# An attention kernel with a long convolution beside it: transfers of at most 128 KB, and rows of k fetched once

## The chip, the cores and the metric

The kernel runs on one core of a Trainium2 chip. The metric is device time in microseconds of one execution. A measurement of a kernel is the median of several runs; the kernel before took 1098.95 us in the median of three (1097.54 to 1100.45).

The core has these engines, named here as the profile names them: PE multiplies matrices (PEld loads its weights), ACT applies functions, DVE does vector arithmetic, POOL and SP do little arithmetic here and issue transfers between the chip's memory and the core. The transfers themselves are moved by 16 DMA engines, which all queues share.

## What is computed

Two independent parts, written side by side into one output.

```python
def _A_ref(x, wq, wk, wv, wo):          # x [1, 2048, 512], 32 heads of 16
    q = heads(x @ wq); k = x @ wk; v = x @ wv      # one k and one v for all heads
    scores = einsum("bhqd,bkd->bhqk", q, k) * 16 ** -0.5
    o = einsum("bhqk,bkd->bhqd", softmax(scores), v)
    return concat_heads(o) @ wo

def _B_ref(q, k, v, shift_k, ssm_k, ssm_D):        # each [1, 2048, 512]
    k_shift = sum(k shifted down by i rows * shift_k[:, i] for i in range(4))
    kv = k_shift * v
    y = causal long convolution of kv with ssm_k, per channel (by FFT) + kv * ssm_D
    return q * y

out = concatenate([a, b], axis=-1)                 # [1, 2048, 1024]
```

## The kernel before, in words

**Attention** runs from the start to the end. Its 1024 tiles are taken in one fixed order by `attend`. For each, PE multiplies scores into a PSUM tile s (L781), ACT takes the exponential into p (L789), and PE multiplies p with v into accumulators f (L801), some tiles later. DVE empties the accumulators into ao every 16 tiles (L817, L818) and SP stores them (od, L820). The queries of the next group of four heads (st) are read back from memory by SP (L748), 20 tiles before they are used.

**The convolution and the projections are filler.** They are written as generators (`conv_pe`, `conv_short`, `conv_dve`, `rest_of_q`, `wo_heads`, `wo_part`). A planner, `_Fill`, lets them put a few instructions behind each attention tile, by credits of PE and DVE time per tile; `yield WAIT, n` makes a generator wait some tiles, as an allowance for a load that it has just issued. The order of every engine's instructions is therefore fixed when the program is built. At run time each engine works through its own list in order and waits on semaphores.

**Where the bytes of the filler go.** The convolution is done as a transform over 2048 positions, split 128 x 16: a row of a tensor is one of 16 positions m, on 128 partitions. Channels are taken in two blocks (blk) of CB = 256.

- `short_load`, `window` and `short_products` make kv of a block in eight steps m2 of two rows. For two rows of output with four taps, five rows of k are needed; `window` fetches those five into one of three buffers inside kk, so that each row of k is fetched two or three times. The first windows reach back before the block's rows 0: those rows are rows 13 to 15 of the partition before, fetched in two pieces, with zeros on partition 0.
- `table` loads the cosines and sines (ff forward, fi backward), 256 KB for each step; `short_products` also loads v, `backward` loads q and stores the result r.
- `long_load` loads hin, the long filter of a block, in two transfers of 1 MB. `long_forward` transforms it.
- All of these are issued by POOL, in the order of its list. A transfer takes the next of eight semaphores in turn (DMASW0 to DMASW7), and waits for the one that had this semaphore before.
- SP issues the attention's transfers and, among them, those of the projections: the store of two quarters of x (xd, L701) and their reload (xT, L737), 1 MB each; the loads of the output weights (wof, L876), of the head outputs and their scales (of, r: L853, L862), and the stores of projected rows (wp, L909). SP and ACT have eight semaphores of their own (DMAHW0 to DMAHW7), used in the same way.

Of the kernel before, what the change touches and what calls it, by code (L numbers as in the profile page):

```python
# [8 lines left out]
F32 = mybir.dt.float32  # L9
# [10 lines left out]
P = 128  # L20
S = 2048
# [75 lines left out]
class _Emit:  # L97
# [160 lines left out]
    def table(self, n, m2):  # L258
        t = self.w.tile([P, 2, 2, P], F32, tag="ft", bufs=FT, name=self.nm(n))
        self.nc.gpsimd.dma_start(t, self.I[n][:, 2 * m2 : 2 * m2 + 2])  # L260
        return t
# [22 lines left out]
    def long_load(self, blk):  # L284

        nc = self.nc
        hin = self.w.tile([P, 2, S], F32, tag="in", bufs=1, name=self.nm("hin"))
        for ct in range(2):
            c0 = blk * CB + ct * P
            nc.gpsimd.dma_start(hin[:, ct, :], self.I["B_ssm_k"][c0 : c0 + P, :])  # L290
        return hin
# [28 lines left out]
    def short_load(self, blk):  # L320
        nc, w = self.nc, self.w
        cs = slice(blk * CB, (blk + 1) * CB)
        tpb = w.tile([P, 4, CB], F32, tag="tp", bufs=1, name=self.nm("tpb"))
        for i in range(4):
            nc.gpsimd.dma_start(tpb[:, i, :], self.skd[i : i + 1, cs].broadcast_to([P, CB]))
        kk = w.tile([P, 3, 5, CB], F32, tag="in", bufs=1, name=self.nm("kk"))
        for m2 in range(2):
            self.window(kk, blk, m2)
        return tpb, kk

    def window(self, kk, blk, m2):

        nc, k, cs = self.nc, kk[:, m2 % 3], slice(blk * CB, (blk + 1) * CB)
        n = max(0, 3 - 2 * m2)
        if n:
            nc.gpsimd.memset(k[0:1, 0:n, :], 0.0)
            for a, b in ((1, 16), (16, P)):
                nc.gpsimd.dma_start(k[a:b, 0:n, :], self.kr[a - 1 : b - 1, 16 - n : 16, cs])
        nc.gpsimd.dma_start(k[:, n:5, :], self.kr[:, 2 * m2 - 3 + n : 2 * m2 + 2, cs])

    def short_products(self, blk, tpb, kk):
# [3 lines left out]
        for m2 in range(8):  # L345
            yield from self.after(*[("x", blk, m2 - AHEAD)] * (m2 >= AHEAD))
            if m2 + 2 < 8:
                self.window(kk, blk, m2 + 2)
            r = slice(2 * m2, 2 * m2 + 2)
            v = self.s2("v")  # L350
            nc.gpsimd.dma_start(v, self.vr[:, r, cs])
# [6 lines left out]
            nc.vector.tensor_tensor(a, kx(3), tap(3), ALU.mult)  # L358
            for i in (2, 1, 0):
                t = self.s2("t")  # L360
                yield 0, 700
                nc.vector.tensor_tensor(t, kx(i), tap(i), ALU.mult)  # L362
                yield 0, 700
                nc.vector.tensor_tensor(a, a, t, ALU.add)  # L364
# [31 lines left out]
    def backward(self, blk, cx, places):  # L396
# [6 lines left out]
        def load(m2):  # L403
            if m2 > 1:
                ft[m2] = self.table("fi", m2)
            q[m2] = self.s2("q")
            nc.gpsimd.dma_start(q[m2], self.qr[:, 2 * m2 : 2 * m2 + 2, cs])
# [4 lines left out]
        for m2 in range(8):  # L412
# [14 lines left out]
            nc.gpsimd.dma_start(self.orr[:, 2 * m2 : 2 * m2 + 2, D + blk * CB : D + (blk + 1) * CB], r)  # L427
# [225 lines left out]
    def prologue(self):  # L653
# [45 lines left out]
        for c in range(2, 4):  # L699
            self.k_rows(c, cut[c])  # L700
            nc.sync.dma_start(self.xd[c - 2], self.xT[c])  # L701
# [8 lines left out]
    def rest_of_q(self):  # L710
# [5 lines left out]
        for c in range(4):  # L716
# [128 lines left out]
    def heads(self, G):  # L845
# [7 lines left out]
        nc.sync.dma_start(o, od[0])  # L853
# [8 lines left out]
        nc.sync.dma_start(r, rows.unsqueeze(1).broadcast_to([8, DH, 512]))  # L862
# [36 lines left out]
    def wo_part(self):  # L899
        nc, w, I = self.nc, self.w, self.I  # L900
        xr = self.out.rearrange("b (c p i) d -> (b c) p i d", c=4, p=P, i=4)
        for c in range(3):
            yield from self.after(("oc", 4 * c + 3))
            for i in (0, 2):
                b = yield from self.wo_rows(i, range(4 * c, 4 * c + 4), 1400)
                for r in range(2):
                    t = self.s2("wp", (512,))
                    nc.vector.tensor_scalar(t, b[r], 1 / (OS * WS), None, ALU.mult)
                    nc.sync.dma_start(xr[c][:, i + r, 0:D], t)  # L909
# [305 lines left out]
```

## Time and profile before

| | |
|---|---|
| median of three runs | 1098.95 us (1097.54 to 1100.45) |
| the profiled execution | 1102.16 us, of which its span is 1100.4 us |
| mean granted clock of PE | 0.986 |
| moved by queue q0 (POOL's transfers) | 40.89 MB, 11.5% of 16 engines' span |
| moved by queue q1 (SP's) | 43.50 MB, 12.4% |
| from issue to landing, median | ff 4.6 us (256 KB), v 5.0 us (256 KB), kk 5.8 us (640 KB), hin 7.9 us (1 MB) |

The profile is taken from one execution. An engine's busy share is an average over stages with different limits: up to about 700 us PE carries attention and filler, from 700 to 850 us ACT is busy without a break, and in the last 250 us both kinds of stretch alternate. In 40 slices of 27.5 us, in tenths of busy time (DMA: of the 16 engines; GB/s: what they moved):

```profile
PE   6798889899999999999997999988888999899886
ACT  3596879799899899999988899999999999999984
DMA  7326432512312111123325422110101331111101
GB/s 230 112 83 203 138 120 64 187 59 70 121 30 68 61 52 59 45 70 120 123 92 172 164 78 71 46 40 20 41 20 31 111 98 50 52 37 30 36 4 42
```

"Issue" in the waits and in the chain is time in which an engine waited for nothing that the profile shows.

### The profile page before, as it was taken

The page shows a single profiled execution, that of the slowest core. Times are in us where ns is not written, and L with a number is a line of the kernel's source. Part 1 is how long each engine was busy: PE and PEld are TensorE (multiplying, and loading weights), DVE is VectorE, ACT ScalarE, POOL GpSimd, SP SyncE. Part 2 cuts the span into 40 slices and gives each one's busy share as a digit, 9 for nine tenths or more (in the row PEclk, how much of TensorE's full clock was granted, in tenths as well). Part 3 has the DMA queues.
Part 4 walks back from the last instruction along what each step waited for, and adds up shares of the span by engine and source line. Part 5 has one row for each costly group of instructions (what it writes and reads, how often), then busy time and mean ns, then how long its engine had stood idle before and what let it go on. Part 6 is the DMA issues. An engine that isn't in the chain of part 4 may idle for free.

```text
span 1100.4 us, 65958 instructions
## 1 busy us (share of the span) xinstructions
PE 988.4 (90%) x30907; PEld 597.8 (54%) x30907; DVE 681.7 (62%) x994; ACT 979.9 (89%) x1038; POOL 104.6 (10%) x158
## 2 busy tenths in 40 slices
PE   6798889899999999999997999988888999899886
PEld 4355556565555665665664566544444666555452
DVE  3755657788589788888877853699995211111132
ACT  3596879799899899999988899999999999999984
POOL 3212211000100000012222200000000210000000
PEclk8999999999999999999999999999999999999998
DMA  7326432512312111123325422110101331111101
GB/s 230 112 83 203 138 120 64 187 59 70 121 30 68 61 52 59 45 70 120 123 92 172 164 78 71 46 40 20 41 20 31 111 98 50 52 37 30 36 4 42
DMA packets 52002, 89.48 MB, mean 81 GB/s; under 512 B 11612, under 2 KB 34186, under 8 KB 50700
## 3 DMA queue, kind: packets, MB, share of 16 engines
q1 hardware_dynamic: 38316, 43.50, 12.4%
q0 software_dynamic: 11648, 40.89, 11.5%
q8 instruction: 243, 3.98, 1.5%
q10 hardware_dynamic: 1760, 0.81, 0.3%
q14 instruction: 35, 0.29, 0.1%
HBM read 60.16 MB, written 25.02 MB: 77 GB/s over the span
## 4 chain that ended last, share of the span: by engine, by line
ACT 45%; PE 36%; issue 11%; DVE 7%; DMA 1%; ACTq 0%; SPq 0%; DVEq 0%
ACT p L789 44%; PE f L801 16%; PE s L781 9%; PE f L221 9%; PE f L306 1%; DVE sp L142 1%; PE f L204 1%; DMA wqf<-in_A_wq 1%; DVE xT L540 1%; DVE gm L651 1%; DVE cut L619 0%; PE x L528 0%; DVE sp L256 0%; DVE gn L640 0%; PE x L204 0%
## 5 line engine op out<-in xcount | busy, mean ns | idle before, releaser
L789 ACT ACTIVATE p<-s 128x1024 f32<-128x1024 f32 x1024 | 968.1, 1050 | 86.0 <-PE s L781 78.3
L801 PE MATMUL f<-p,vx 64*32 64x256 f32 x16384 | 667.7, 377 | 12.9 <-issue 12.7
L781 PE MATMUL s<-st,kst 49*32 49x512 f16 x8192 | 474.3, 383 | 64.0 <-ACT p L789 36.8
L801 PEld LDWEIGHTS f<-p,vx 64*32 64x32 f32 x16384 | 343.8, 107 | 111.9 <-issue 23.7
L781 PEld LDWEIGHTS <-kst 49*32 49x32 f16 x8192 | 188.1, 91 | 269.7 <-issue 199.6
L817 DVE COPY ao<-f 128x256 f32<-128x256 f32 x64 | 27.0, 422 | 157.0 <-PE f L801 156.9
L142 DVE TENSOR_TENSOR sp<-sp 128x1024 f32<-128x1024 f32 x96 | 111.3, 1215 | 0.0
L256 DVE COPY sp<-f 128x512 f32<-128x512 f32 x64 | 41.2, 686 | 69.7 <-PE f L221 69.5
L221 PE MATMUL f<-xT,wq 64*32 64x512 f16 x1344 | 69.5, 379 | 3.6 <-issue 2.1
L221 PE MATMUL f<-wo,o 64*32 64x512 f16 x1440 | 71.7, 376 | 1.2 <-DVE cut L619 0.8
L221 PE MATMUL f<-a,ff 64*32 64x256 f32 x1024 | 54.1, 383 | 4.1 <-DVE cut L619 2.1
L142 DVE TENSOR_TENSOR sp<-sp,sp 128x1024 f32<-128x1024 f32 x48 | 56.0, 1218 | 0.2
L221 PE MATMUL f<-hT,ff 64*32 64x256 f32 x1024 | 46.5, 376 | 1.9 <-issue 1.8
L221 PE MATMUL f<-sp,fi 64*32 64x256 f32 x1024 | 46.1, 376 | 0.0
L260 POOL DMA_DIRECT2D ff<-in_ff x32 | 17.5, 549 | 268.7 <-PE s L781 248.8
L426 DVE TENSOR_TENSOR r<-f,q 128x256 f32<-128x256 f32 x32 | 12.1, 419 | 41.1 <-PE f L221 41.1
L427 POOL DMA_DIRECT2D out<-r x16 | 11.5, 717 | 262.0 <-DVE r L426 256.2
L221 PEld LDWEIGHTS <-o 64*32 64x32 f16 x1440 | 27.6, 92 | 15.4 <-issue 3.7
L221 PEld LDWEIGHTS <-wq 64*32 64x32 f16 x1344 | 26.2, 93 | 17.7 <-issue 4.5
L221 PEld LDWEIGHTS f<-a,ff 64*32 64x32 f32 x1024 | 24.8, 106 | 17.1 <-issue 3.3
L364 DVE TENSOR_TENSOR a<-a,t 128x512 f32<-128x512 f32 x48 | 33.2, 691 | 1.5
L362 DVE TENSOR_TENSOR t<-kk,tpb 128x512 f32<-128x512 f32 x48 | 32.8, 683 | 0.0
(138 smaller groups left out, 620.9 us busy)
## 6 DMA issues: line engine op xcount, KB each, us to landing
ff<-in_ff POOLq DMA_DIRECT2D x32, 256.0 KB, 4.6
od<-ao SPq DMA_DIRECT2D x60, 128.0 KB
kk<-in_B_k POOLq DMA_DIRECT2D x12, 640.0 KB, 5.8
qd<-qp SPq DMA_DIRECT2D x48, 128.0 KB
st<-qd SPq DMA_DIRECT2D x60, 98.0 KB
v<-in_B_v POOLq DMA_DIRECT2D x16, 256.0 KB, 5.0
hin<-in_B_ssm_k POOLq DMA_DIRECT2D x4, 1024.0 KB, 7.9
fi<-in_fi POOLq DMA_DIRECT2D x16, 256.0 KB, 4.0
```

What stands on the lines that cost most here:

```text
L142: v.tensor_tensor(part(out), part(a), part(b), op)
L221: self.nc.tensor.matmul(out[j : j + 32, cols], w[r, j : j + 32], x[r], start=half == m == 0, stop=half == 1 and m == k - 1,)
L256: self.nc.vector.tensor_copy(c[:, :, m + i, :], b[i].rearrange("p (q n) -> p q n", q=2))
L260: self.nc.gpsimd.dma_start(t, self.I[n][:, 2 * m2 : 2 * m2 + 2])
L362: nc.vector.tensor_tensor(t, kx(i), tap(i), ALU.mult)
L364: nc.vector.tensor_tensor(a, a, t, ALU.add)
L426: nc.vector.tensor_tensor(r[:, i, :], b[i][:, cols], q[m2][:, i, :], ALU.mult)
L427: nc.gpsimd.dma_start(self.orr[:, 2 * m2 : 2 * m2 + 2, D + blk * CB : D + (blk + 1) * CB], r)
L781: self.nc.tensor.matmul(s[j : j + 32, e, :], self.kst[rows, k * P + j : k * P + j + 32], self.st[n][rows, :, 256 * h : 256 * h + 256], sta ...
L789: self.nc.scalar.activation(p, s, AF.Exp, scale=DH**-0.5 / SC / SC)
L801: nc.tensor.matmul(self.acc[e][32 * j : 32 * j + 32, 0:256], self.vx[rows, k, :], self.pt[x][rows, j % 2, 256 * (j // 2) : 256 * (j // 2) ...
L817: nc.vector.tensor_copy(a, self.acc[0][:, 0:256])
```

## The change

Every transfer of the filler that carried more than 128 KB is issued in pieces of at most 128 KB. Rows of k get fixed places: kk has 16 rows of CB, the three shifted rows are first put into places 13 to 15, and each step fetches its own two rows. The products read rows by their number modulo 16; where the two rows of a product are rows 15 and 0, it is done in two halves. Rows 13 to 15 of the block itself arrive later in the places of the shifted ones. The order of work on PE, ACT and DVE is otherwise the same.

```diff
     def table(self, n, m2):
         t = self.w.tile([P, 2, 2, P], F32, tag="ft", bufs=FT, name=self.nm(n))
-        self.nc.gpsimd.dma_start(t, self.I[n][:, 2 * m2 : 2 * m2 + 2])
+        for i in range(2):
+            self.nc.gpsimd.dma_start(t[:, i], self.I[n][:, 2 * m2 + i])
...
-            nc.gpsimd.dma_start(hin[:, ct, :], self.I["B_ssm_k"][c0 : c0 + P, :])
+            for i in range(0, S, CB):
+                nc.gpsimd.dma_start(hin[:, ct, i : i + CB], self.I["B_ssm_k"][c0 : c0 + P, i : i + CB])
...
-        kk = w.tile([P, 3, 5, CB], F32, tag="in", bufs=1, name=self.nm("kk"))
+        kk = w.tile([P, 16, CB], F32, tag="in", bufs=1, name=self.nm("kk"))
+        nc.gpsimd.memset(kk[0:1, 13:16, :], 0.0)
+        for i in range(13, 16):
+            for a, b in ((1, 16), (16, P)):
+                nc.gpsimd.dma_start(kk[a:b, i, :], self.kr[a - 1 : b - 1, i, cs])
         for m2 in range(2):
-            self.window(kk, blk, m2)
+            self.rows(kk, blk, m2)
...
-    def window(self, kk, blk, m2):
-
-        nc, k, cs = self.nc, kk[:, m2 % 3], slice(blk * CB, (blk + 1) * CB)
-        n = max(0, 3 - 2 * m2)
-        if n:
-            nc.gpsimd.memset(k[0:1, 0:n, :], 0.0)
-            for a, b in ((1, 16), (16, P)):
-                nc.gpsimd.dma_start(k[a:b, 0:n, :], self.kr[a - 1 : b - 1, 16 - n : 16, cs])
-        nc.gpsimd.dma_start(k[:, n:5, :], self.kr[:, 2 * m2 - 3 + n : 2 * m2 + 2, cs])
+    def rows(self, kk, blk, m2):
+        for i in (2 * m2, 2 * m2 + 1):
+            self.nc.gpsimd.dma_start(kk[:, i, :], self.kr[:, i, blk * CB : (blk + 1) * CB])
...
             if m2 + 2 < 8:
-                self.window(kk, blk, m2 + 2)
+                self.rows(kk, blk, m2 + 2)
             r = slice(2 * m2, 2 * m2 + 2)
             v = self.s2("v")
-            nc.gpsimd.dma_start(v, self.vr[:, r, cs])
+            for i in range(2):
+                nc.gpsimd.dma_start(v[:, i], self.vr[:, 2 * m2 + i, cs])
...
-            kx = lambda i: kk[:, m2 % 3, 3 - i : 5 - i, :]
-            tap = lambda i: tpb[:, i : i + 1, :].broadcast_to([P, 2, CB])
+            tap = lambda i, n: tpb[:, i : i + 1, :].broadcast_to([P, n, CB])
+
+            def product(out, i):
+                r = 2 * m2 - i
+                for n, x in ((slice(0, 1), slice(15, 16)), (slice(1, 2), slice(0, 1))) if r == -1 else ((slice(0, 2), slice(r % 16, r % 16 + 2)),):
+                    nc.vector.tensor_tensor(out[:, n], kk[:, x], tap(i, n.stop - n.start), ALU.mult)
+
             yield 0, 700
-            nc.vector.tensor_tensor(a, kx(3), tap(3), ALU.mult)
+            product(a, 3)
...
-            nc.sync.dma_start(self.xd[c - 2], self.xT[c])
+            for i in range(8):
+                nc.sync.dma_start(self.xd[c - 2, :, i // 4, i % 4], self.xT[c][:, i // 4, i % 4])
...
-                self.nc.sync.dma_start(self.xT[c + 2], self.xd[c])
+                for i in range(8):
+                    self.nc.sync.dma_start(self.xT[c + 2][:, i // 4, i % 4], self.xd[c, :, i // 4, i % 4])
```

In the same way, without being shown: q and the store of r in `backward` in two pieces each, of and r in `heads` in two, and the stores of wp in `wo_part` in two.

How the lists of the issuing engines change, at two places. In these rows, "waits" names the semaphores that the instruction waits for: DMASWn and DMAHWn are earlier transfers, the others are counters of engines.

On POOL, at steps 0 to 2 of the first block's short products (kk rows of k, v rows of v), before:

```order
L339 DMA kk_1315<-in_B_k 128x5x256 [waits DMASW4_49]
L351 DMA v_1615<-in_B_v 128x2x256 [waits DMAHW0_49,DMAHW2_49,DMASW5_49,DVE_49]
L339 DMA kk_1315<-in_B_k 128x5x256 [waits DMASW6_49,DVE_49,Pool_49]
L351 DMA v_1947<-in_B_v 128x2x256 [waits DMAHW2_49,DMASW7_49]
L339 DMA kk_1315<-in_B_k 128x5x256 [waits DMASW0_49,DMASW1_49,DVE_49,Pool_49]
```

and now:

```order
L339 DMA kk_1329<-in_B_k 128x256 [waits DMASW2_49]
L339 DMA kk_1329<-in_B_k 128x256 [waits DMASW3_49]
L352 DMA v_1642<-in_B_v 128x256 [waits DMAHW1_49,DMAHW0_49,DMAHW2_49,DMASW4_49,DVE_49]
L352 DMA v_1642<-in_B_v 128x256 [waits DMASW5_49]
L339 DMA kk_1329<-in_B_k 128x256 [waits DMASW6_49]
L339 DMA kk_1329<-in_B_k 128x256 [waits DMASW7_49]
L352 DMA v_1977<-in_B_v 128x256 [waits DMAHW0_49,DMASW0_49,DVE_49]
L352 DMA v_1977<-in_B_v 128x256 [waits DMASW1_49]
```

Five rows of k in one transfer have become two transfers of a row each, v two transfers, and kk no longer waits for DVE. POOL's list has 313 rows in place of 168.

On SP, at the end of the prologue (xd is the store of x, wof, dt and sk are small loads behind it, gn a row of the queries' tile in memory), before:

```order
L701 DMA xd<-xT 128x4096 [waits DMAHW2_49,Activation_49]
L701 DMA xd<-xT 128x4096 [waits DMAHW3_49,Activation_49]
L876 DMA wof_492<-in_A_wo 128x512 [waits DMAHW4_49,Pool_49]
L269 DMA dt<-in_B_ssm_D 128x4x1 [waits DMAHW5_49]
L271 DMA sk<-in_B_shift_k 128x4x4 [waits DMAHW6_49,DVE_49]
```

and now, with the first and the last of the 16 pieces of xd:

```order
L710 DMA xd<-xT 128x512 [waits DMAHW2_49,Activation_49]
L710 DMA xd<-xT 128x512 [waits DMAHW3_49]
...
L710 DMA xd<-xT 128x512 [waits DMAHW0_49]
L710 DMA xd<-xT 128x512 [waits DMAHW1_49]
L888 DMA wof_506<-in_A_wo 128x512 [waits DMAHW2_49,Pool_49]
L270 DMA dt<-in_B_ssm_D 128x4x1 [waits DMAHW3_49]
L272 DMA sk<-in_B_shift_k 128x4x4 [waits DMAHW4_49,DVE_49]
```

The loads wof, dt and sk now stand behind 16 issues in place of two. The reload of x (xT) puts eight issues in place of one ahead of a load of st.

More of the change, by code (lines that the diff above doesn't have):

```diff
@@ L406, in load @@
             q[m2] = self.s2("q")
[L407 removed]
+            for i in range(2):
+                nc.gpsimd.dma_start(q[m2][:, i], self.qr[:, 2 * m2 + i, cs])
         load(0)
@@ L861, in heads @@
         rows = self.rd[G].rearrange("(h m) x -> h (m x)", h=8)
-        nc.sync.dma_start(r, rows.unsqueeze(1).broadcast_to([8, DH, 512]))
+        for i in range(0, 512, CB):
+            nc.sync.dma_start(r[:, i : i + CB], rows[:, i : i + CB].unsqueeze(1).broadcast_to([8, DH, CB]))
         yield WAIT, 4
```

11 lines of the change are left out of this document (7 added, 4 removed).

## The prediction

> **What bounds the kernel now.** I read the page first: busy times and the chain of work that ended last, then the waits by engine, then the chain in order of time, and at its longest gaps the windows and the DMA queues.
>
> ```profile
> PE 988.4 (90%) x30907; PEld 597.8 (54%) x30907; DVE 681.7 (62%) x994; ACT 979.9 (89%) x1038; POOL 104.6 (10%) x158
> ACT 45%; PE 36%; issue 11%; DVE 7%; DMA 1%; ACTq 0%; SPq 0%; DVEq 0%
> q0 software_dynamic: 11648, 40.89, 11.5%
> q8 instruction: 243, 3.98, 1.5%
> ```
>
> PE and ACT share the chain; POOL and SP, which issue every transfer that this change cuts, are not on it. So the change can reach the time only through a wait that it takes from PE, ACT or DVE, or gives to them. A row of a queue reads packets, MB, share: queue q8 moved 243 packets of 16 KB (3.98 MB / 243) while PE ran 2 x 30,907 = 61,814 instructions, 254 to a packet. I take q8 for PE's own instruction stream. Next, what PE waited for when no semaphore held it:
>
> ```profile
> PE f L801 <- issue: 12.7, 11, 3.2
> PE f L221 <- issue: 7.1, 5, 2.2
> PE s L781 <- issue: 5.0, 4, 2.5
> 51.98 2.12 issue
> 88.57 2.61 issue
> 142.26 2.26 issue
> 199.81 2.55 issue
> 284.77 1.69 issue
> 559.60 1.22 issue
> 594.56 3.20 issue
> 625.63 1.00 issue
> 1057.38 2.24 issue
> 1050.00:1075.00 25.00, 21.80 (x680) 14.90 (x679) 8.88 (x22) 19.99 (x22) 0.00 (x0) 0.93 0.01 3
> ```
>
> The first three rows are total us, times, longest: 12.7 + 7.1 + 5.0 = 24.8 us of PE standing without a cause that the profile names. The two-number rows are the long ones in the chain itself (start, length). The one at 1057 is something else: the window under it, which reads its length, then PE, PEld, DVE, ACT and POOL busy, PE's granted clock, DMA share and GB/s, has no transfers to speak of (share 0.01). So 22.6 us are left. What happens around one of them:
>
> ```profile
> 139.00:140.00 1.00, 1.00 (x51) 0.65 (x40) 0.96 (x3) 0.88 (x2) 0.07 (x1) 1.00 1.03 389
> 143.00:144.00 1.00, 0.00 (x0) 0.00 (x0) 0.96 (x3) 0.41 (x1) 0.00 (x0) 1.00 0.05 8
> 145.00:146.00 1.00, 1.00 (x33) 0.77 (x25) 0.97 (x2) 0.00 (x0) 0.73 (x1) 0.59 0.09 16
> q0 software_dynamic: 368, 1.33, 79.5%
> q8 instruction: 2, 0.03, 3.7%
> ```
>
> The DMA engines are full at 139 (share 1.03); PE stops at 142.26 and starts again at 144.52. The q0 row is the queue from 137 to 142, in which q8 had no packet at all; the q8 row is 142 to 146. PE's next block of instructions waited behind POOL's 1.33 MB. **So bursts of data make PE's instructions late**, and the clock then falls for some us (0.59 in the last window). The same pattern stands at all eight long gaps: they follow the bursts that POOL issues (kk, v, ff, hin), three of them together with a 1 MB transfer of SP (51.98 xd, 88.57 and 199.81 xT).
>
> **The change, part by part.**
>
> *POOL's transfers in pieces.* What one issue costs POOL:
>
> ```profile
> 136.35 0.87 POOL L339 DMA_DIRECT2D kk<-in_B_k  x1 [11.82 <-DVE t L362]
> 137.96 1.11 POOL L260 DMA_DIRECT2D ff<-in_ff  x2
> 191.42 1.07 POOL L290 DMA_DIRECT2D hin<-in_B_ssm_k  x2 [13.40 <-DVE t L362]
> 77.69 2.39 POOL L325 DMA_DIRECT2D tpb<-skd  x4 [43.94 <-DMA skd<-tps]
> tpb<-skd POOLq DMA_DIRECT2D x8, 128.0 KB, 3.7
> ```
>
> An issue costs 0.53 to 0.60 us whether it carries 128 KB (tpb) or 1 MB (hin); only a longer pattern costs more (kk 0.87). In pieces of 128 KB, POOL therefore sends at most 131 KB per 0.55 us, 238 GB/s, against the 389 GB/s that full engines moved above, 61%: POOL alone can no longer fill them. Issues rise by 145 (the instruction lists have 313 rows for POOL against 168, headings included), 145 x 0.55 = 80 us more on an engine that is busy 105 of 1100 us. What hides it is POOL's own idle time, 995 us, and the lead with which loads are asked for, two steps by the code. Without that cover a step of the short products would pay 6 x 0.55 = 3.3 us for kk, v and ff instead of at least 0.87 + 2 x 0.56 = 2.0 us, 1.3 us per step, 21 us over 16 steps; I take nothing of it.
>
> *Rows of k once.* Each block fetched 5 rows eight times, 40 rows of 128 KB; now 16 and the three shifted ones, 19. That is 21 x 131 KB x 2 = 5.5 MB of q0's 40.9 MB less, all of it in the stretches with the long gaps. It also takes away the wait of kk for its third buffer (11.82 us in the row above), behind which v and ff stood on POOL's queue. DVE gets four multiplications (0.69 us, L358 below) in two halves each: nothing.
>
> *SP's transfers in pieces.*
>
> ```profile
> 43.20 0.90 SPq L701 DMA_DIRECT2D xd<-xT  x2
> 44.19 1.96 SPq L876 DMA_DIRECT2D wof<-in_A_wo  x1
> 75.24 0.35 SPq L820 DMA_DIRECT2D od<-ao  x1
> 52.54 0.43 DVE L239 TENSOR_SCALAR wo<-wof 128x512 f16<-128x512 f32 x1 [4.14 <-DMA wof<-in_A_wo]
> 56.90 0.42 DVE L817 COPY ao<-f 128x256 f32<-128x256 f32 x1 [2.61 <-PE f L801]
> ```
>
> The xd store becomes 16 issues. At the 0.35 us of od, the nearest row with 128 KB, they hold SP for 5.6 us instead of 0.9, so wof leaves near 49 instead of 44. But wof had waited behind those 2 MB anyway (DVE was held for it until 52.54), and the bytes ahead of it are the same; I expect it between 52 and 54, and DVE's next work is bound to PE at 56.9: 3 to 4 us of cover, and beyond that each us is DVE's and, through the accumulators that L817 empties, PE's. The xT reloads put 8 x 0.35 = 2.8 us ahead of the next head group's st, which is issued 20 tiles, of 0.94 us of ACT each (979.9 / 1038), before it is read. At 131 KB per 0.35 us SP can still fill the engines (375 GB/s), but every transfer waits for the one eight before it on its semaphore, so at most 8 x 131 KB = 1 MB stands in its queue: I keep half of these gaps.
>
> *What the gaps are worth.* Five long ones behind POOL's bursts alone: 2.26 + 1.69 + 1.22 + 3.20 + 1.00 = 9.37 us, of which I let 85% go, 8.0. Three with SP: 2.12 + 2.61 + 2.55 = 7.28, half, 3.6. The other 22.6 - 16.65 = 5.95 us are short ones, half, 3.0. And the slow clock behind three of them:
>
> ```profile
> 90.00:95.00 5.00, 3.82 (x94) 2.69 (x100) 1.10 (x3) 1.94 (x2) 0.40 (x1) 0.66 1.02 332
> 145.00:150.00 5.00, 5.00 (x136) 3.87 (x121) 0.98 (x2) 2.91 (x3) 2.05 (x3) 0.66 0.69 214
> 200.00:210.00 10.00, 7.63 (x205) 4.47 (x213) 3.77 (x6) 5.75 (x7) 0.54 (x1) 0.83 0.64 234
> ```
>
> 5 x 0.34 + 5 x 0.34 + 10 x 0.17 = 5.1 us of full clock lost, 3.0 regained. Sum 17.6 us. PE is not always what ACT waits for next: where PE comes sooner it meets DVE (7% of the chain, and the short products are DVE's). I take 0.7 of it, 12.3 us; the bounds are 0.3 and 1.
>
> *More semaphores.* The instruction lists name 71 more waited-for semaphores on PE, since a half table lands by itself.
>
> ```profile
> L221 PEldq EVENT_SEMAPHORE  x55: 51/51/2797, 48.4 to 1059.6; - x55
> ```
>
> 51 ns each would be 3.6 us if each took an instruction on PE and none fell into a wait; below, 0. I take 1.8. Net 12.3 - 1.8 = 10.5 us. The profiled execution took 1102.16 us with a span of 1100.4, 3.2 us above the median of the three runs, 1098.95; 1102.16 - 10.5 = 1091.7 on its own scale, **1098.95 - 10.5 = 1088.5 us** on that of the median.
>
> Two pages speak against the mechanism. The Trainium skill, "Runtime: NRT & Kernel Launch", section "Instruction fetch mechanics", says that a queue refills instructions in blocks of 16 KiB and that the cost of crossing a block is mostly hidden; the trace agrees on the block (16 KB) and not on the hiding (2.26 us in which PE stood). The Trainium skill, "DMA: Bandwidth & Descriptors", section "Queues, rings and completion order", says that a DMA engine goes round the queues packet by packet; by that rule a block would wait for one data packet, some 3.6 KB (1.33 MB / 368), not for a burst, and cutting bursts would gain nothing. The five us without a q8 packet speak for the burst.
>
> **The rivals.** *Nothing gained.* The block is late for a reason that pieces don't touch (it takes its turn among packets, and these are as many as before), or the time found at the gaps is waited for again at DVE. For it: the gap at 1057 shows that PE also stops with no transfers about, and DVE is 0.96 busy beside the gap at 142. Against it: the eight others all follow a burst, and from 700 to 850, where little is moved, there is none. At pass-through 0.3 and half the gaps gone, 0.3 x 11 = 3.3, less 1.8 to 3.6 for semaphores: 1098.95 - 0.5, about 1098.5.
>
> *The rings stay full, and POOL is paced by them: slower.* Place: the first load of the short convolution, from 80 us, when SP's xT pieces (375 GB/s) and POOL's (238) together exceed what drains.
>
> ```profile
> kk<-in_B_k POOLq DMA_DIRECT2D x1, 640.0 KB, 10.5
> v<-in_B_v POOLq DMA_DIRECT2D x1, 256.0 KB, 7.6
> 89.39 0.69 DVE L358 TENSOR_TENSOR a<-kk,tpb 128x512 f32<-128x512 f32 x1 [6.30 <-DMA kk<-in_B_k]
> L221 PE MATMUL f<-a,ff x1024: 372/376/632, 105.8 to 697.3; 64*32 64x256 f32 x171
> ```
>
> 18 pieces (6 edges, 6 rows, 4 of ff, 2 of v) go out eight at a time; if each lands after L us, v's last piece lands at 80.7 + 18 L / 8 + L. DVE must have it about 1.4 us before 105.8, when PE first reads a: it decides from L = 7.3 us on (23.7 / 3.25). Landings of 7.6 to 10.5 us in that stretch speak for it, the 3.7 us of a 128 KB piece against. At L = 9 v lands at 110, PE waits 5.6 us; the full rings keep the gaps too, so nothing is regained, and the semaphores cost 1.8: 1098.95 + 7.4 = 1106.
>
> **How the numbers follow.** Forecast 0.67, nothing gained 0.17, full rings 0.16. The forecast's own range, from pass-through 0.4 with 3.6 us of semaphores to all but nothing left of 22.6 + 5.1 us at 0.85, is 3.4 to 22 us of gain: 1077 to 1095.5. The full rings reach 1106 and half of that case lies below 1103, so the range that leaves 2 in 10 out is 1078 to 1103. About 0.3% (3.3 us) is what a measurement of this kernel tells from no change: 1095.6 and 1102.3 are the marks. Faster: nearly all of the forecast and a little of the second case, 0.68. Same: most of the second case and the edge of the others, 0.15. Slower: 0.17.
>
> **What would show it.** Right: q0 below 70% of the engines in the windows of POOL's bursts (79.5% above, waits included); the PE waits on "issue" fall from 24.8 to about 10 us; at 142, 285 and 595 no gap over 1 us; granted clock back at 1.00 from 145 to 150; q0 near 35 MB; kk on POOL no longer waiting for DVE's t. Wrong: gaps of 2 us that stay although the share falls (then the block is not late because of the burst); issues of POOL above 0.7 us; DVE's first product after 90 us; ACT's wait for PE's scores unchanged although PE's gaps went.

## The result, and the profile after

| | before | after |
|---|---|---|
| median | 1098.95 us (1097.54 to 1100.45) | 1085.98 us (1085.49 to 1085.99) |
| ratio, 95% interval | | 0.988 (0.9858 to 0.9903) |
| profiled execution | 1102.16 us | 1085.98 us |

The change saves 12.97 us between the medians; 1088.5 was forecast. The two profiled executions differ by 16.2 us, because the one of before was 3.2 us above its median.

The page after: busy times by engine, then queue q0 (packets, MB, share of 16 engines).

```profile
PE 981.9 (91%) x30907; PEld 597.1 (55%) x30907; DVE 681.9 (63%) x998; ACT 979.5 (90%) x1038; POOL 165.9 (15%) x300
q0 software_dynamic: 13152, 35.40, 10.8%
```

POOL issues 142 instructions more (300 against 158) and is busy 61 us longer; PE and ACT wait for none of its loads, and DVE's waits for them did not grow: v 1.2 and kk 6.3 us before, v 2.9 and kk 0.7 after, and 5.3 before its first product that the profile puts down to a reload of xT. q0 carries 40.89 - 35.40 = 5.5 MB less. PE, ACT and DVE have the work they had, and PE's clock fell about as often (between 36 and 700 us, three times for some 1.7 us of full clock each, before and after). So the time came from waits. The waits of after, in us, times, longest:

```profile
PE f L811 <- issue: 6.2, 6, 2.0
PE f L221 <- issue: 5.9, 4, 2.9
ACT p L799 <- PE s L791: 56.6, 86, 4.0
```

and ACT's wait for the scores before:

```profile
ACT p L789 <- PE s L781: 78.3, 101, 7.6
```

PE's waits without a named cause fell from 24.8 to 6.2 + 5.9 = 12.1 us. The two ACT rows fell by 21.7 us, but not all of that is a gain: ACT's first exponential waits for the start of the kernel in both, and the profile names PE as what ended this wait before and a transfer into st after:

```profile
37.62 11.22 ACT L789 ACTIVATE p<-s 128x1024 f32<-128x1024 f32 x12 [7.56 <-PE s L781]
37.47 11.21 ACT L799 ACTIVATE p<-s 128x1024 f32<-128x1024 f32 x12 [7.48 <-DMA st<-gn]
```

Without it ACT's waits for scores fell by 14.1 us (78.3 - 7.56 - 56.6), and all of its idle time before exponentials from 86.0 to 71.6. The long gaps that are left in the chain of after (start, length):

```profile
95.14 2.04 issue
201.50 1.93 issue
582.20 2.93 issue
1042.74 2.31 issue
```

The first two are those of 88 and 199 before, behind the reloads of xT. The third is the one of 594 before: the program runs 11 us ahead by then, and this gap has hardly shrunk. The engines' share in the 4 us before it is 0.78, where it was 0.83. The fourth is the one at 1057, which has no transfers about. The gaps of 52, 142, 285, 560 and 626 are gone. In the chain of after there is also a stretch of "issue" from 501 to 572 in pieces of up to 20 us. It is not PE's: the chain runs there along POOL's queue, where stores of r stand behind DVE, so the shares of the two chains can't be set side by side.

The place of the old gap at 142, in the windows of after (length; PE, PEld, DVE, ACT and POOL busy; PE's clock; DMA share; GB/s):

```profile
125.00:130.00 5.00, 4.70 (x149) 2.94 (x141) 4.50 (x9) 4.26 (x6) 2.99 (x6) 1.00 0.54 163
130.00:135.00 5.00, 4.40 (x152) 2.68 (x145) 3.88 (x7) 4.67 (x6) 1.24 (x3) 1.00 0.63 192
135.00:140.00 5.00, 5.00 (x192) 3.34 (x184) 4.90 (x9) 4.82 (x6) 0.00 (x0) 1.00 0.09 28
```

The load that filled the engines to 1.03 at 389 GB/s now runs some us earlier at 0.54 to 0.63 and 163 to 192 GB/s, and PE goes through at full clock. What that is worth can be read between two stores of od, the same two in both kernels, with 552 matmuls of PE and 17 instructions of ACT between them, before and then after:

```profile
133.55:153.00 19.45, 17.04 (x552) 11.24 (x540) 13.03 (x21) 15.27 (x17) 4.92 (x7) 0.91 0.48 159
131.70:147.37 15.67, 15.46 (x552) 9.89 (x553) 13.06 (x21) 15.22 (x17) 2.12 (x4) 1.00 0.21 65
```

The stretch is 3.78 us shorter: the gap of 2.26 us is gone, and with it some 1.75 us that PE lost to a clock of 0.91 on average.

The one new stall is at SP's pieces of xd. SP's timeline, DVE's, and two windows of after:

```profile
43.04 9.13 SPq L710 DMA_DIRECT2D xd<-xT  x16
52.26 2.02 SPq L888 DMA_DIRECT2D wof<-in_A_wo  x1
```

```profile
56.66 0.43 DVE L239 TENSOR_SCALAR wo<-wof 128x512 f16<-128x512 f32 x1 [8.41 <-DMA wof<-in_A_wo]
```

```profile
50.00:55.00 5.00, 5.00 (x196) 3.42 (x181) 0.00 (x0) 4.88 (x6) 0.00 (x0) 1.00 0.46 144
55.00:60.00 5.00, 2.32 (x61) 0.82 (x52) 3.17 (x7) 3.02 (x4) 0.00 (x0) 0.96 0.49 110
```

and the same two windows of before:

```profile
50.00:55.00 5.00, 2.88 (x116) 1.56 (x101) 1.71 (x3) 2.72 (x4) 0.00 (x0) 1.00 0.56 151
55.00:60.00 5.00, 4.58 (x165) 2.89 (x157) 2.48 (x5) 5.00 (x6) 0.00 (x0) 1.00 0.19 50
```

Sixteen pieces held SP for 9.13 us, 0.57 each; wof, whose four loads of 256 KB stay whole in the kernel after, reached DVE at 56.66 instead of 52.54. The gap of PE at 52 went, and PE stood for wof instead: 7.46 us busy in these ten before, 7.32 after.

### The profile page after: what moved, and what is told of

Read it like the earlier page. It is cut to its first block, busy times and chain, and to the rows that moved or that the text cites. A ratio compares the mean times of both kernels' runs of the same rounds, so it can differ in the third digit from the quotient of the medians.

```text
span 1084.2 us, 66263 instructions
## 1 busy us (share of the span) xinstructions
PE 981.9 (91%) x30907; PEld 597.1 (55%) x30907; DVE 681.9 (63%) x998; ACT 979.5 (90%) x1038; POOL 165.9 (15%) x300
## 3 DMA queue, kind: packets, MB, share of 16 engines
q1 hardware_dynamic: 48156, 43.51, 12.8%
q0 software_dynamic: 13152, 35.40, 10.8%
## 4 chain that ended last, share of the span: by engine, by line
ACT 44%; PE 30%; issue 15%; DVE 5%; DMA 3%; POOL 2%; SPq 0%; ACTq 0%; POOLq 0%; DVEq 0%
ACT p L799 44%; PE f L811 13%; PE s L791 7%; PE f L221 7%; PE f L308 1%; POOL out L435 1%; DVE sp L142 1%; DMA wqf<-in_A_wq 1%; POOL fi L261 1%; PE x L536 1%; DMA qd<-qp 1%; DVE cut L627 0%; POOL q L414 0%; DVE xT L548 0%; DMA wof<-in_A_wo 0%
## 5 line engine op out<-in xcount | busy, mean ns | idle before, releaser
L799 ACT ACTIVATE p<-s 128x1024 f32<-128x1024 f32 x1024 | 967.8, 1050 | 71.6 <-PE s L791 56.6
L811 PEld LDWEIGHTS f<-p,vx 64*32 64x32 f32 x16384 | 343.2, 107 | 103.9 <-issue 14.1
L221 PE MATMUL f<-xT,wq 64*32 64x512 f16 x1344 | 73.2, 378 | 1.7 <-DVE gm L659 1.5
L221 PE MATMUL f<-wo,o 64*32 64x512 f16 x1440 | 71.1, 375 | 1.2 <-DVE cut L627 0.7
L261 POOL DMA_DIRECT2D ff<-in_ff x64 | 34.0, 537 | 244.5 <-PE s L791 235.1
L221 PE MATMUL f<-a,ff 64*32 64x256 f32 x1024 | 53.1, 383 | 6.8 <-issue 3.6
L435 POOL DMA_DIRECT2D out<-r x32 | 17.5, 550 | 243.2 <-DVE r L433 243.2
L221 PE MATMUL f<-hT,ff 64*32 64x256 f32 x1024 | 46.3, 376 | 0.0
L221 PE MATMUL f<-sp,fi 64*32 64x256 f32 x1024 | 43.6, 376 | 0.2 <-DVE r L433 0.2
L433 DVE TENSOR_TENSOR r<-f,q 128x256 f32<-128x256 f32 x32 | 12.1, 419 | 40.1 <-PE f L221 40.1
L221 PEld LDWEIGHTS <-wq 64*32 64x32 f16 x1344 | 28.1, 93 | 14.6 <-DVE gm L659 2.2
L221 PEld LDWEIGHTS f<-a,ff 64*32 64x32 f32 x1024 | 24.6, 106 | 20.2 <-issue 5.0
L221 PEld LDWEIGHTS <-o 64*32 64x32 f16 x1440 | 27.0, 92 | 15.4 <-issue 2.8
L352 POOL DMA_DIRECT2D v<-in_B_v x32 | 17.0, 536 | 107.9 <-PE s L791 50.0
```

Of the source, the lines that this page charges most:

```text
L221: self.nc.tensor.matmul(out[j : j + 32, cols], w[r, j : j + 32], x[r], start=half == m == 0, stop=half == 1 and m == k - 1,)
L261: self.nc.gpsimd.dma_start(t[:, i], self.I[n][:, 2 * m2 + i])
L352: nc.gpsimd.dma_start(v[:, i], self.vr[:, 2 * m2 + i, cs])
L433: nc.vector.tensor_tensor(r[:, i, :], b[i][:, cols], q[m2][:, i, :], ALU.mult)
L435: nc.gpsimd.dma_start(self.orr[:, 2 * m2 + i, D + blk * CB : D + (blk + 1) * CB], r[:, i])
L799: self.nc.scalar.activation(p, s, AF.Exp, scale=DH**-0.5 / SC / SC)
```

## The experiments

Each run was timed in turn with the kernel before on the same chip; ratios are to that. Executions of one kernel scatter by several us (before: 1099.88 to 1107.54 beside the first four runs, 1097.48 to 1111.35 beside the copies), so verdicts rest on ratios and on places within a profile, not on one profile's end.

### Parts of the change

Rows of k alone, on the kernel before (two rows in a transfer, all else whole):

```diff
-        kk = w.tile([P, 3, 5, CB], F32, tag="in", bufs=1, name=self.nm("kk"))
+        kk = w.tile([P, 16, CB], F32, tag="in", bufs=1, name=self.nm("kk"))
...
+    def rows(self, kk, blk, m2):
+        nc = self.nc
+        nc.gpsimd.dma_start(kk[:, 2 * m2 : 2 * m2 + 2, :], self.kr[:, 2 * m2 : 2 * m2 + 2, blk * CB : (blk + 1) * CB])
```

> The kernel before, with rows of k fetched once into fixed places, but two rows to a transfer (256 KB) and every other transfer whole. If the gain comes from k itself (5.5 MB less, no wait for the third buffer), most of the 13 us should be here: 1086 to 1089. If it comes from bursts that are cut into pieces, the long filter, the x transfers and the tables still burst, and a step still sends 0.79 MB in about 2 us: the gaps at 52, 88, 200 and 285 us stay (9 us together) and 1092 to 1096 is measured. If rows of k do nothing: 1099.

POOL's pieces alone, on the kernel before (tables, v, q, r and hin cut as in the change; the windows of five rows and SP's transfers as before):

> The kernel before, with tables, v, q, the store of r and the long filter in pieces of 128 KB on POOL; k still in windows of five rows (640 KB), SP's transfers whole. By bursts: the long filter's gaps (285 us, part of 200 us) go, the k windows' gaps shrink since only 640 KB come at once: 1090 to 1094. By k alone: no change, 1097 to 1100.

Both of them, that is the kernel after with SP's transfers of x whole again (rows of k stay single, and the smaller pieces of SP, of, r and wp, stay too):

```diff
-            for i in range(8):
-                nc.sync.dma_start(self.xd[c - 2, :, i // 4, i % 4], self.xT[c][:, i // 4, i % 4])
+            nc.sync.dma_start(self.xd[c - 2], self.xT[c])
...
-                for i in range(8):
-                    self.nc.sync.dma_start(self.xT[c + 2][:, i // 4, i % 4], self.xd[c, :, i // 4, i % 4])
+                self.nc.sync.dma_start(self.xT[c + 2], self.xd[c])
```

> The changed kernel, with the store and the reload of x whole again (1 MB each). Theory that SP's sixteen pieces cost (0.57 us each, the output weights land 4 us later, DVE waits 8.4 us for them and PE 2.3): the first 77 us come back to the kernel before, 2 us earlier, the gap of 2 us at 52 returns with it; 1083 to 1086 in all, depending on the gaps at 88 and 200 us. Theory that every transfer in pieces helps: 1088 to 1092.

The kernel after with the pieces of xd on POOL's queue:

```diff
-                nc.sync.dma_start(self.xd[c - 2, :, i // 4, i % 4], self.xT[c][:, i // 4, i % 4])
+                nc.gpsimd.dma_start(self.xd[c - 2, :, i // 4, i % 4], self.xT[c][:, i // 4, i % 4])
```

> The changed kernel, with the sixteen pieces of the x store issued by POOL, which has nothing to do from 34 to 80 us, in place of SP. If SP's issues are what makes the output weights late: these land by 50 us, DVE does not wait for them, no gap of PE at 52, and the whole run is 2 to 5 us shorter than the changed kernel: 1081 to 1084. If the weights are late because of the bytes ahead of them: no change, 1086.

| | median, us | ratio, 95% interval |
|---|---|---|
| before, beside these four | 1104.9 | |
| rows of k alone | 1097.57 | 0.9925 (0.9896 to 0.9955) |
| POOL's pieces alone | 1097.45 | 0.9933 (0.9909 to 0.9958) |
| both, x whole | 1089.77 | 0.9862 (0.9835 to 0.989) |
| all, xd by POOL | 1085.84 | 0.9842 (0.9811 to 0.9873) |

The two halves of the change add up within their intervals: 0.75% + 0.67% = 1.42%, and both together gave 1.38%. Each profile shows its own part (start and length of gaps in the chains): rows of k alone have none left over 1 us at 142 and 200 and keep 3.16 us at 89.41, 2.22 at 280.26 and 3.75 at 592.65; POOL's pieces alone keep 1.44 at 142.51, 1.16 at 207.04 and 1.27 at 289.93, and 3.43 at 89.08 and 3.21 at 594.38. With x whole again a gap stands at 49.38 (1.73 us), as was expected. SP's pieces of x add nothing that can be told: with x whole 0.9862, with all pieces 0.988 (not timed beside these) and, xd by POOL, 0.9842, and all three intervals overlap. On DVE's timeline with xd on POOL's queue, the two products of wo stand without a wait for wof:

```profile
50.19 0.41 DVE L239 TENSOR_SCALAR wo<-wof 128x512 f16<-128x512 f32 x1
57.26 0.42 DVE L239 TENSOR_SCALAR wo<-wof 128x512 f16<-128x512 f32 x1
```

So the stall at wof came from the order on SP's queue. At 75 us it is worth 2.6 us (the second store of od starts at 74.82 instead of 77.40); how much of that reaches the end the intervals don't tell, so the 2 to 5 us expected are not shown.

### Reloads of xT at another time

The kernel after with xd on POOL's queue, and the two reloads of xT moved on, away from the loads of the convolution (from 81 to 122 us and from 189 to 297 us in the profiles of the two kernels):

```diff
+                if g == 2 and late is not None:
...
+                        self.nc.sync.dma_start(self.xT[late + 2][:, i // 4, i % 4], self.xd[late, :, i // 4, i % 4])
...
-                for i in range(8):
-                    self.nc.sync.dma_start(self.xT[c + 2][:, i // 4, i % 4], self.xd[c, :, i // 4, i % 4])
+                late = c
```

> The changed kernel, with the x store issued by POOL and each reload of x issued about 100 us later, in front of the next quarter's second half, where neither the first rows of k nor the long filter are being fetched. If what is left of the gaps at 95 and 201 us comes from SP's and POOL's pieces adding up: both shrink below 1 us and the run is 2 to 4 us shorter than with the x store on POOL alone. If they come from POOL's pieces alone: no change.

Measured: 1082.53 us beside 1101.15, ratio 0.9814 (0.9779 to 0.9849), the lowest of all, but its interval overlaps that of the kernel it changes (0.9811 to 0.9873), so the 2 to 4 us expected are not shown. SP's timeline shows where the reloads went, and PE's waits what is left:

```profile
121.50 3.81 SPq L732 DMA_DIRECT2D xT<-xd  x8
...
296.53 4.94 SPq L732 DMA_DIRECT2D xT<-xd  x8
```

```profile
PE f L815 <- issue: 7.2, 11, 2.0
PE f L221 <- issue: 4.8, 6, 2.3
PE s L795 <- issue: 0.8, 2, 0.5
```

The gaps at 95 and 201 are gone; the longest before 640 us is 0.9 us. The sum of the waits did not fall (12.8 us), but this profile is of the longest of its six executions (1088.42; the others 1079.32 to 1084.14). It was not timed side by side with the kernel after; its interval lies below that kernel's (0.9858 to 0.9903).

### Copies put where there was no gap

The kernel before, with four copies of 2 MB from one place of the device's memory to another, between 325 and 440 us, started by POOL: whole (two of 1 MB, rows of 8 KB), in pieces of 128 KB, and whole with rows of 1 KB.

```diff
+    def burst(self, n):
+        src = self.od[n - 7 : n + 1].rearrange("n (p r) x -> (n p) (r x)", r=4)
...
+            self.nc.gpsimd.dma_start(self.bs[P * j : P * j + P, 0:2048], src[P * j : P * j + P])
```

> The kernel before, with four extra bursts between 340 and 440 us, where it has no gap: each copies 2 MB of the head outputs to a scratch place in memory, by POOL, in two transfers of 1 MB with rows of 8 KB. If a burst makes PE's instructions late: a gap of 1.5 to 3 us behind each of the four, 6 to 10 us in all, 1105 to 1109. If gaps have another cause: 1099.

> The same four copies in pieces of 128 KB (16 issues of 0.55 us each, rows of 1 KB). By bursts: the engines are never full, no gap over 1 us, 1099 to 1101. By bytes alone: as with whole transfers, 1105 to 1109.

> The same four copies in two transfers of 1 MB each, but in rows of 1 KB as in the pieces. Tells the size of a packet from the pace of the issue: if the block of instructions waits for what was queued before it, the gaps are as with rows of 8 KB, 1104 to 1109; if it takes its turn packet by packet and only long packets hold it, they are gone, 1099 to 1101.

| | median, us | ratio, 95% interval |
|---|---|---|
| before, beside these | 1101.15 | |
| whole | 1111.46 | 1.0114 (1.0058 to 1.0171) |
| pieces | 1112.06 | 1.0097 (1.0064 to 1.0129) |
| whole, rows of 1 KB | 1111.87 | 1.0101 (1.0044 to 1.0157) |

The last median is of three executions; a fourth took 5259.16 us, and no profile shows why. The whole copies do make gaps where before had none: behind three of the four, 2.05 to 2.54 us long. In the windows around the second copy, with the gap itself from 362.93 to 365.47:

```profile
359.00:363.00 4.00, 3.93 (x142) 2.48 (x119) 4.00 (x4) 4.00 (x6) 0.00 (x0) 1.00 0.99 374
363.00:367.00 4.00, 1.52 (x33) 1.12 (x40) 2.60 (x3) 0.88 (x1) 0.00 (x0) 0.83 0.49 167
```

But the three don't differ in time, and the premise of the pieces failed: a copy of 128 KB lands after 5.2 us, eight are under way, so the engines stayed at 0.72 to 0.87 of their time. PE's waits on "issue" from 300 to 460 us were 7.5 us (whole), 3.8 (pieces) and 4.7 (whole, rows of 1 KB), against 0.7 in the kernel before, so the times don't follow these waits alone. This told that a burst costs, and not why. The next four were made of loads.

### Extra loads: how fast they are handed over, or how long the rows are

The kernel before, with the second block's long filter loaded over itself eight more times between 310 and 440 us, 16 MB in all, whenever DVE has filled an ao (a small copy on POOL times it). Four ways of handing over the same bytes:

```diff
+        for ct in range(2):
+            nc.gpsimd.dma_start(self.hin1[:, ct, :], src[CB + ct * P : CB + ct * P + P, :])
```

> The kernel before, with the second block's long filter loaded eight more times over itself (16 MB in all, once for each od store from about 310 to 420 us, started by POOL when DVE has filled ao), each time as two transfers of 1 MB with rows of 8 KB. It adds loads and leaves the results as they are. The kernel before has no gap of PE over 1 us in this stretch. Bursts make PE's instructions late: gaps of 1 to 3 us behind most of the eight, engines full for some 5 us each, 8 to 16 us in all, 1107 to 1115. Size of the row decides (8 KB in a row keep a packet of instructions waiting longer): the same here. Nothing gained, PE stands for another reason: no gaps, within 3 us of before.

```diff
+            for i in range(0, S, CB):
+                nc.gpsimd.dma_start(self.hin1[:, ct, i : i + CB], src[CB + ct * P : CB + ct * P + P, i : i + CB])
```

> The same eight extra loads, each in 16 pieces of 128 KB with rows of 1 KB, as the change cuts them. Pace of issue decides: POOL hands over 128 KB per 0.55 us, so the engines stay below about 0.7 of their time, gaps under 1 us, 0 to 4 us in all. Size of the row decides: the same, 0 to 4 us. Number of packets decides (eight times as many in the way as with 8 KB rows): more gaps than with the whole loads.

```diff
+            for i in range(2):
+                rows = lambda t: t.rearrange("p (j i x) -> p i j x", i=2, x=CB)[:, i]
+                nc.gpsimd.dma_start(rows(self.hin1[:, ct, :]), rows(src[CB + ct * P : CB + ct * P + P, :]))
```

> The same eight extra loads as four transfers of 512 KB each, all with rows of 1 KB (even and odd blocks of 256 columns apart). The rows are as short as in the pieces, but 2 MB are handed over in about 2 us. Pace of issue decides: gaps as with the whole loads, 8 to 16 us. Size of the row decides: as with the pieces, 0 to 4 us.

```diff
+            for j in range(0, P, 16):
+                nc.gpsimd.dma_start(self.hin1[j : j + 16, ct, :], src[CB + ct * P + j : CB + ct * P + j + 16, :])
```

> The same eight extra loads in 16 pieces of 128 KB, each 16 partitions with whole rows of 8 KB. The rows are as long as in the whole loads, but POOL hands over 128 KB per 0.55 us. Pace of issue decides: as with the pieces of short rows, 0 to 4 us. Size of the row decides: as with the whole loads, 8 to 16 us.

Before beside them: 1099.89 us. In the table, "PE without cause" is the sum of PE's waits on "issue" from 300 to 460 us (0.7 us in the kernel before), and q0's share is of the same 160 us.

| | median, us | ratio, 95% interval | PE without cause, us | q0: MB, share |
|---|---|---|---|---|
| 2 x 1 MB, rows of 8 KB | 1122.98 | 1.0199 (1.0146 to 1.0252) | 14.3 | 17.83, 30.4% |
| 16 pieces, rows of 1 KB | 1117.72 | 1.0159 (1.0124 to 1.0193) | 10.4 | 17.83, 37.7% |
| 4 x 512 KB, rows of 1 KB | 1125.82 | 1.0227 (1.019 to 1.0265) | 16.1 | 17.83, 35.1% |
| 16 pieces of 16 partitions, rows of 8 KB | 1156.3 | 1.0495 (1.0457 to 1.0533) | 26.2 | 14.52, 56.9% |

The whole loads took 1122.98 us, above the 1107 to 1115 expected, while their waits (14.3 us) lie within the 8 to 16 expected of the gaps.

**The size of the row falls as a cause.** With short rows handed over at once the gaps are as many as with long rows, not fewer. (In the trace the rows of 1 KB go four to a packet: most packets of the extra loads are 4096 bytes and took 0.16 to 0.18 us in the median, with rows of 8 KB 8192 bytes and 0.31 us. So packets were tried at two sizes, a factor of two apart.) The chains, long rows first, then short (four of the gaps each; start, length):

```profile
354.88 1.65 issue
373.05 1.72 issue
408.14 2.89 issue
428.14 2.19 issue
```

```profile
355.38 2.20 issue
375.78 1.66 issue
412.20 2.32 issue
430.11 1.59 issue
```

**A slower pace helps, but only by a part.** Pieces of the same short rows cost 17.8 us instead of 25.9, about a third less (the two intervals touch at 1.019), where almost nothing was expected to be left. Against the whole loads with long rows the intervals overlap, and only the waits differ, 10.4 us against 14.3. What remains is seen in the kernel with pieces, in its chain, in the window of 4 us before that gap, and in the queues from 330 to 336.9:

```profile
334.56 2.37 issue
```

```profile
330.56:334.56 4.00, 3.82 (x104) 1.52 (x89) 3.86 (x8) 4.00 (x5) 2.67 (x6) 1.00 0.85 206
```

```profile
q0 software_dynamic: 400, 1.08, 62.1%
q1 hardware_dynamic: 368, 0.39, 20.1%
```

POOL alone keeps the engines at 0.62; SP's stores of qd take another 0.20, and the two together are enough.

**The gaps go with full engines.** The fourth kernel was meant to be slow at handing over, and its pieces landed so late that POOL was held and the engines were full all the same. Its issues, and a window of 4 us about the start of its gap of 3.58 us at 322.67:

```profile
hin<-in_B_ssm_k POOLq DMA_DIRECT2D x112, 128.0 KB, 7.4
```

```profile
319.50:323.50 4.00, 3.17 (x111) 1.84 (x89) 2.11 (x4) 3.43 (x4) 2.00 (x5) 1.00 1.04 133
```

Full engines at 133 GB/s, and the most gaps of all: that speaks for the engines' time, and not for the bytes or the rows. As a test of pace against rows this kernel failed, since its premise (engines below capacity) did not hold; part of its loss is also that the attention's own small loads came late. Over eight of the profiles (before, after, after with xd by POOL, the same with xT later, and these four), 72 gaps of over 1 us stand in the chains beside the one near the end, and 65 of them follow 4 us in which the engines were busy for at least 0.75; in the kernel before, only 20 of the 166 windows of 4 us from 36 to 700 us are as full as that, and 31 to 48 with the extra loads. Full engines do not always make a gap: the kernel after has 15 such windows and three gaps. And one of the eight long gaps of before, at 559.60, follows 4 us at only 0.48.

**The gaps stand at the borders of PE's instruction blocks.** The trace does not name the instructions that PE waits for, but they can be counted. When the eight long gaps of the kernel before begin, PE's queue has started 1217, 3265, 6081, 9409, 14529, 31425, 33473 and 35265 records (matmuls, weight loads and a few others) since the start of the trace. Each of these numbers is 193 above a multiple of 256, and a packet of q8 carries 254 instructions on average. Of the 72 gaps of the eight profiles, 71 stand at such a place; the gap near the end of before does not (60,425 is 9 above). At each of the eight, a packet of q8 ends 1.2 to 1.6 us before PE goes on. The packet itself took 0.96 to 1.24 us, but it began 5.0 to 8.0 us after the packet before it, where the median of all is 4.1. So PE stood for its next block, and what was late is the start of that block's packet, not the packet itself.

### What a microsecond of these gaps is worth

All profiles, PE's waits on "issue" against the profiled execution's time:

| | PE without cause, us | time, us |
|---|---|---|
| all, xd by POOL | 11.6 | 1082.84 |
| after | 12.1 | 1085.98 |
| the same as the first, xT later | 12.8 | 1088.42 |
| both halves, x whole | 16.1 | 1089.82 |
| rows of k alone | 22.6 | 1103.84 |
| before | 24.8 | 1102.16 |
| POOL's pieces alone | 27.9 | 1106.54 |
| copies: pieces; whole; short rows | 30.2; 30.5; 30.5 | 1110.69; 1107.89; 1108.77 |
| extra loads: pieces | 36.5 | 1120.32 |
| extra loads: whole | 41.0 | 1126.15 |
| extra loads: short rows | 42.4 | 1127.91 |
| extra loads: 16 partitions | 63.3 | 1165.13 |

A straight line through all but the last is 1068.6 + 1.38 x waits, with no point further off than 3.9 us (the last lies 9 us above it). The kernels differ in other things too, so this is a relation between them and no proof, and it rests on one execution of each; but it holds for kernels that had gaps added as for those that lost some. It also shows why single profiles mislead: the two halves of the change look no better than before in their profiles, which are of the longest of seven executions each (1090.62 to 1103.84, and 1091.66 to 1106.54).

## Why the prediction was right, point by point

**What bounds the kernel, and the mechanism: right.** The gain came out of PE's waits without a named cause, in most of the places named, and adding bursts where there was no gap made gaps. That these are waits for PE's instructions, which the prediction took from the absence of q8, the count of instructions at the gaps bears out. One reading in it was too wide: that all eight long gaps follow a burst does not hold for the one at 559.60 (share 0.48). And its first sign of being wrong, gaps of 2 us that stay although the share falls, is near at 582: a gap of 2.93 us stayed, but the share before it had fallen only from 0.83 to 0.78. The two pages quoted against it: that the cost of crossing a block is mostly hidden (the Trainium skill, "Runtime: NRT & Kernel Launch", section "Instruction fetch mechanics") holds here in the main while the engines are not full: 0.7 us of such waits from 300 to 460 us in the kernel before, 10.4 to 26.2 with the extra loads. The rule of turns packet by packet (the Trainium skill, "DMA: Bandwidth & Descriptors", section "Queues, rings and completion order") is not disproved, but a wait of one data packet, as the profile counts them, does not explain gaps of 2 us at any row size tried (0.16 to 0.18 us a packet of 4 KB, 0.31 of 8 KB, in the median). Why a full engine starts the block's packet late no run here shows.

**The waits that go: a little too many.** Predicted 8.0 + 3.6 + 3.0 = 14.6 us, measured 24.8 - 12.1 = 12.7. By parts: the five behind POOL's bursts alone kept the one at 582, 2.93 of 9.37 us, so 69% went and not 85%. There the engines are at 0.78 in the 4 us before, since POOL hands over 18 transfers almost without a break from 571 to 582, and q1 moves besides. The three with SP kept 2.04 + 1.93 of 7.28 us, about the half that was said, but the one at 52, which went, was given back at wof. The short ones kept 12.1 - 2.04 - 1.93 - 2.93 - 2.31 = 2.9 of 5.95, the half that was said.

**The pass-through: too low, the step that was mis-sized.** I took 0.7 of 17.6 us, of which 3.0 were clock. The clock gave nothing back: it fell three times between 36 and 700 us before (behind the gaps of 88, 142 and 199) and three times after (behind the stall at wof and the gaps of 95 and 582: 0.96 and 0.70 in the windows of 5 us from 55 to 65, 0.72 and 0.94 from 95 to 105, 0.66 from 585 to 590), some 5.1 us of full clock in both. So 12.7 us went, all waits, and 12.97 us came out between the medians, 16.2 between the two profiled executions: 1.0 to 1.3 for each us of wait, where the sum had 12.3 / 14.6 = 0.84. ACT's idle time before exponentials fell by 14.4 us. The line through all profiles gives 1.38, but it is of kernels in which the clock differs too. What came through besides the waits the runs don't separate. That 1088.5 lies so near to 1085.98 is in part luck: fewer waits gone, no clock regained and a higher pass-through nearly cancelled.

**POOL's issues: right.** On the groups of after (busy, mean ns of one):

```profile
L261 POOL DMA_DIRECT2D ff<-in_ff x64 | 34.0, 537 | 244.5 <-PE s L791 235.1 <-PE f L221 7.0 <-DMA kk<-in_B_k 1.7
L339 POOL DMA_DIRECT2D kk<-in_B_k x32 | 17.1, 540 | 3.1 <-DMA ff<-in_ff 1.8 <-DMA kk<-in_B_k 1.3
```

0.54 us each, and kk waits for no work of DVE any more (54.6 us of POOL's waits for t before). v waits there instead (28.7 us for DVE's a), and its lead is a little smaller: in the first load DVE waits 2.88 us for v, which it did not before (PE first reads a 0.6 us later than before).

**Rows of k once: costed as bytes, worth half of the gain.** The prediction gave them no term of their own. Alone they made 0.75%, as much as all of POOL's pieces. Whether by the 5.5 MB or by the wait of kk that went the runs don't separate.

**SP's pieces: the price was wrong.** 0.35 us was taken from od, which is issued alone; sixteen in a row cost 0.57. wof landed 4.1 us later than before and not at 52 to 54, the cover to 56.9 was used up, and the next stores of od are 1.4 us (59.29 against 57.88) and 2.2 us (77.40 against 75.24) late before the gains begin. The reloads of xT cost 3.72 and 4.74 us for eight, 0.47 and 0.59 each.

**Semaphores: not settled.** On L221's row, PE's waits of their own rise from 55 to 95:

```profile
L221 PEldq EVENT_SEMAPHORE  x95: 51/51/3123, 48.3 to 1045.1; - x95
```

That is 40 x 51 ns = 2.0 us on this line at most, near the 1.8 taken for all; what of it reaches the end no run separates.

**The rivals.** Nothing gained: fell, with the ratio. Full rings: in part, and without the harm. In the first load the engines were full for 5 us, the clock fell behind the gap at 95, and DVE waited for v:

```profile
90.00:95.00 5.00, 4.26 (x128) 2.58 (x128) 3.70 (x8) 4.20 (x5) 2.67 (x5) 1.00 1.02 273
95.00:100.00 5.00, 2.96 (x58) 1.92 (x63) 2.08 (x4) 1.10 (x2) 4.24 (x8) 0.72 0.75 235
99.62 0.69 DVE L372 TENSOR_TENSOR a<-a,v 128x512 f32<-128x512 f32 x1 [2.88 <-DMA v<-in_B_v]
```

But pieces of kk landed after 4.7 us in the median and ff after 6.4, below the 7.3 from which this rival decides, and PE first read a at 106.4 instead of 105.8. The sign that was to speak for it did show too, DVE's first product after 90 us:

```profile
90.49 0.69 DVE L361 TENSOR_TENSOR a<-kk,tpb 128x512 f32<-128x512 f32 x1 [5.30 <-DMA xT<-xd]
```

It is late because all of that stretch started late (POOL's issue of tpb at 80.06 instead of 77.69, behind the xd pieces), not because the load takes longer: 10.4 us from tpb to the product, 11.7 before. As a sign it was badly chosen, since it measured the time since the start and not the length of the stretch.

## What to carry to other kernels

Where an engine works through tens of thousands of instructions, look for waits that no semaphore explains, count the instructions up to them, and lay them beside the DMA engines' share in the us before: if they stand a fixed number of instructions apart and the engines were full, move or slow the transfers, even those that nobody waits for. It is the sum over all queues that counts, so a big load is best put where the other queue is idle (that took away the gaps at 95 and 201 here, though the run's time can't be told from the one before it); fetching fewer bytes and dropping a wait gained as much here as cutting POOL's other transfers. Before cutting, price the issues on the queue that carries them as a row of issues and not as one alone, and look at what stands behind them.

## What the hardware showed that I had not expected

- PE's waits for instructions fall on the same place in every block of 256: 71 of 72 gaps begin after a number of records that is 193 above a multiple of 256.
- Rows of 1 KB took more of the engines' time, as the profile books it, than rows of 8 KB: 37.7% or 35.1% against 30.4% of 160 us for the same 17.83 MB, so cutting along the row cost 15 to 24% more of it.
- Pieces that touch only 16 partitions took 56.9% for 14.52 MB, 2.3 times as much per MB as whole transfers with the same rows of 8 KB, and landed after 7.4 us instead of the 4.1 us of pieces over 128 partitions. The Trainium skill, "DMA: Bandwidth & Descriptors", section "Rules for kernel authors", asks for 128 partitions and at least 1 MiB in a transfer for the highest bandwidth; these runs agree on the partitions. On the size, the highest bandwidth was not what this kernel needed.
- The same issue on SP cost 0.35 us alone, 0.47 to 0.59 in rows of eight loads and 0.57 in a row of sixteen stores.
